# Seven small products for four of sixteen first-layer blocks per token group, and plain outputs for units 5 to 7

## The chip, the cores and the metric

The kernel runs on one core of a Trainium2 chip. The metric is the device time of one execution in microseconds (us). Before the change the median of 9 runs is 290.35 us, the lowest 289.78, the highest 291.69.

## What is computed

Retention (a linear attention with decay) over 8 batches, 8 heads, 576 positions and a head width of 64, followed by two matrix products with a leaky ReLU between them:

```
scores = q @ k^T / sqrt(64)
ret    = scores * D          # D[i,j] = gamma_h ** (i-j) for i >= j, else 0
x      = (ret @ v), heads side by side          # 4608 tokens x 512
h      = x @ w_in                               # 512 -> 2048
g      = max(0.01 * h, h)
out    = g @ w_out                              # 2048 -> 512
```

Inputs and output are float32; the kernel's matmuls take float16 operands and sum in float32.

## The kernel before, in words

**Units.** The tokens are cut into 36 units of 128 (two chunks of 64 positions). For each unit three tiles (k, q, v) are loaded; ScalarE casts k (`cast_k`, L170), VectorE or GpSimd multiply q and v by a decay table while they cast (`cast_q` L174, `cast_v` L177). q and k are transposed, for the first 8 units on TensorE (`transpose_pe`, `transposed`), later by a transposing DMA on SyncE's queue (`transpose_dma`, L181). `scores` (L209) makes the in-chunk scores and the chunk's state contribution; `masks` (L234) and `state` (L245) are VectorE's; `state_cast` (L273) makes the float16 state.

**Two forms of the outputs.** `outputs_acc` (L312) adds the in-chunk part and the part from the state in PSUM, in four rounds with a drain between, and ScalarE copies the sum into `xT` (`x_copy`, L346). `outputs` (L286) writes the two parts side by side; ScalarE copies one out (`own`, L359), and VectorE adds the other and writes `xT` (`add`, L365).

**Groups.** Four units are one group of 512 tokens (9 groups). `xT[g]` holds x transposed, 4 blocks of 128 features by 512 tokens. The first layer gives 16 blocks of 128 rows of `g`; one is `h_block` (L395): 4 matmuls of 512 columns (L379, in `h_mm`), then ScalarE's leaky ReLU (L393). `h_half` (L400) and `h_unit` (L407) make the same in pieces, for 256 and 128 tokens, while the first groups' units come in.

**The second layer.** Group 0's is written plainly (`wide`, L425, matmuls L429), with two output tiles `osb` of 256 tokens, stored by SyncE (`store`, L417). For groups 1 to 8, `seven` (L475) does it in Winograd's form of Strassen's scheme: tokens, hidden features and output columns are each halved, seven products (L493, 16 matmuls of 256 columns each) take the place of eight. The sums of the weights are made once (`mix_weights`, L446), those of `g` for every group by VectorE (`mix`, L461, instructions L473). The products p1, p6, p5 and p7 take a PSUM bank each, in this order; results are combined by `keep` (L502: ScalarE copy L505, VectorE sums L507) and `give` (L509: ScalarE copy L517, VectorE sums L519), which write two `osb` tiles per group.

**PSUM.** All of first layer, second layer and TensorE transposes share one pool of 4 banks (`acc_pool`, L80), handed out in turn; a bank's next user waits until the last reader of the one before is done. Scores and outputs have a tile each of their own.

**Order.** Every engine runs its instructions in the order in which the program writes them. There is no planner: the order is the text's. In the prologue (L600 to L646) fillers (`keep_warm`, L556: matmuls on a zero tile, nobody reads them) stand where TensorE waits. Then units 3 to 7 come in between pieces of groups 0 and 1 (L716 to L784). `burst(u)` (L682) is `scores(u)`, `outputs(u-1)`, `masks`, `state`, GpSimd's `state_cast`, `own(u-1)`, `add(u-1)`; `ahead(u)` (L697) is the three casts (q and v on GpSimd) and the transposing DMA; `step(u)` (L710) is `burst(u)`, the load of unit u+4 and `ahead(u+2)`. The main loop (L808 to L823) runs for groups 2 to 8: 16 blocks with a step after the 5th and the 13th and half of the mixes after the 9th, the other mixes, and `seven` with a step after its first and its fifth product.

**SyncE's queue.** Loads from unit 8 on, transposing DMAs and stores go out on it in program order.

Of the kernel before, what the change touches and what calls it, by code (L numbers as in the profile page):

```python
# [18 lines left out]
def kernel(  # L19
# [9 lines left out]
    nc = tc.nc  # L29
# [3 lines left out]
    P = 128  # L33
    CH = 64
    BLK = 256
    NP = H // 2
# [5 lines left out]
    HF, HN, HT = NF // 2, DM // 2, TOK // 2  # L42
# [30 lines left out]
    x_pool = ctx.enter_context(tc.tile_pool(name="xp", bufs=3))  # L73
    g_pool = ctx.enter_context(tc.tile_pool(name="gp", bufs=2))
    s_pool = ctx.enter_context(tc.tile_pool(name="sp", bufs=1))
    o_pool = ctx.enter_context(tc.tile_pool(name="op", bufs=3))
    m_pool = ctx.enter_context(tc.tile_pool(name="mp", bufs=1))
    sc_pool = ctx.enter_context(tc.tile_pool(name="scp", bufs=1, space=PSUM))
    ot_pool = ctx.enter_context(tc.tile_pool(name="otp", bufs=1, space=PSUM))
# [24 lines left out]
    w_in16 = const_pool.tile([P, NP, DFF], F16, name="w_in16")  # L104
    w_out16 = const_pool.tile([P, NF, DM], F16, name="w_out16")
    w_mix = const_pool.tile([P, 4, HF, HN], F16, name="w_mix")
    zst = const_pool.tile([P, NP, CH], F16, name="zst")
    idle = const_pool.tile([P, TOK], F16, name="idle")

# [9 lines left out]
    def load(u, eng=None, after=None):  # L119
        for x in (1, 0, 2):  # L120
            t = ld_pool.tile([P, H, D], FP, name=f"t32_{x}")
            t32[u, x] = t
            c = 2 * u
            same = c % CB + 1 < CB
            e = eng[x] if isinstance(eng, dict) else eng or nc.sync
            engs = e if isinstance(e, tuple) else (e,)
            n = H // len(engs)
            for j, rows in ((0, P),) if same else ((0, CH), (1, CH)):
                b, w = (c + j) // CB, (c + j) % CB
                for i, e in enumerate(engs):  # L130
                    hs = slice(n * i, n * i + n)
                    d = e.dma_start(
                        out=t[CH * j : CH * j + rows, hs],
                        in_=(q, k, v)[x][b, hs, CH * w : CH * w + rows, :].rearrange(
                            "h t d -> t h d"
                        ),
                    )
                    if after is not None and (x in after or not isinstance(after, dict)):
                        behind(d, *(after[x] if isinstance(after, dict) else after))
                        after = None  # L140
                    last_load[u, x] = d
# [32 lines left out]
    def cast_q(u, eng):  # L174
        eng.tensor_tensor(out=qk16[u][:, 0], in0=t32[u, 0], in1=decay(u, 0), op=MUL)  # L175

    def cast_v(u, eng):  # L177
        v16[u] = a_pool.tile([P, H, D], F16, name="v16")
        eng.tensor_tensor(out=v16[u], in0=t32[u, 2], in1=decay(u, 1), op=MUL)  # L179
# [54 lines left out]
    def masks(u):  # L234
        s16s[u] = b_pool.tile([P, 2, NP, CH], F16, name="s16")
        nc.vector.tensor_tensor(  # L236
            out=s16s[u],
            in0=sc_tiles[u][:, :, 0],
            in1=mask_sb.unsqueeze(1).unsqueeze(1).to_broadcast([P, 2, NP, CH]),
            op=MUL,  # L240
        )
# [117 lines left out]
    def own(u):  # L359
        owns[u] = b_pool.tile([P, NP, 2, CH], FP, name="own")  # L360
        nc.scalar.copy(  # L361
            out=owns[u], in_=ot_tiles[u][:, :, 0:NP].rearrange("q j c t -> q c j t")
        )
# [23 lines left out]
    def g_tile(g):  # L387
        if g not in g_t:
            g_t[g] = g_pool.tile([P, NF, TOK], F16, name="gt")
        return g_t[g]  # L390

    def leaky(out, in_):
        nc.scalar.activation(out=out, in_=in_, func=mybir.ActivationFunctionType.Lrelu)  # L393

    def h_block(g, f):  # L395
        hps = acc_pool.tile([P, 1, TOK], FP, name="acc")
        h_mm(hps, 0, g, f, slice(0, TOK))
        leaky(g_tile(g)[:, f : f + 1, :], hps)

    def h_half(g, a, fb):  # L400
        ts = slice(a * HT, (a + 1) * HT)
        hps = acc_pool.tile([P, 2, HT], FP, name="acc")
        for n in range(2):
            h_mm(hps, n, g, 2 * fb + n, ts)
        leaky(g_tile(g)[:, 2 * fb : 2 * fb + 2, ts], hps)

    def h_unit(u, fb):  # L407
        g, t0 = u // 4, (u % 4) * P
        ts = slice(t0, t0 + P)
        hps = acc_pool.tile([P, 4, P], FP, name="acc")  # L410
        for n in range(4):
            h_mm(hps, n, g, 4 * fb + n, ts)
        leaky(g_tile(g)[:, 4 * fb : 4 * fb + 4, ts], hps)

    def store(g, a, osb):  # L417
        r0 = g * TOK + a * HT
        nc.sync.dma_start(
            out=out[r0 : r0 + HT, :].rearrange("(t p) d -> p t d", p=P), in_=osb  # L420
        )
# [24 lines left out]
    def mix_weights(n, x):  # L446
        fs = slice(x * HF // 2, (x + 1) * HF // 2)
        a, b = (
            (w_part(0, 1), w_part(0, 0)),
            (w_part(1, 1), w_mix[:, 0]),  # L450
            (w_part(1, 1), w_part(0, 1)),
            (w_part(1, 0), w_mix[:, 1]),
        )[n]
        nc.vector.tensor_tensor(out=w_mix[:, n, fs], in0=a[:, fs], in1=b[:, fs], op=SUB)  # L454
# [101 lines left out]
    def keep_warm(n):  # L556
        t = acc_pool.tile([P, 1, TOK], FP, name="acc")
        for _ in range(n):
            nc.tensor.matmul(out=t[:, 0, :], lhsT=idle[:, 0:P], rhs=idle, start=True, stop=True)
# [76 lines left out]
    cast_q(3, nc.vector)  # L636
    cast_v(3, nc.vector)
    turn_act(3, 0)
    keep_warm(2)
    masks(2)  # L640
    scores(3)
    state_last(2)
# [6 lines left out]
    def halves(g, *items):  # L649
        for a, fb in items:  # L650
            h_half(g, a, fb)

    def cast_qv(u):
        cast_q(u, nc.vector)
        cast_v(u, nc.vector)

    def turn(u, x):
        transpose_pe(u, x)
        transposed(u, x, dve_copy)

# [36 lines left out]
    def ahead(u):  # L697

        if u >= NU:
            return  # L700
        cast_k(u)
        cast_q(u, nc.gpsimd)
        cast_v(u, nc.gpsimd)
        transpose_dma(u)
# [5 lines left out]
    def step(u):  # L710
        burst(u)
        fetch(u + 4)
        ahead(u + 2)


    halves(0, (0, 0), (0, 1))  # L716
    finish2(3)
    state_cast(3, act_copy, (1,))
    halves(0, (0, 2), (0, 3))
# [19 lines left out]
    scores(5)  # L739
    settle(5)  # L740
    cast_k(6)
    cast_qv(6)
    halves(0, (0, 6), (0, 7))
    finish(5)
    halves(0, (1, 6))
    turn(6, 1)
    cast_k(7)
    halves(0, (1, 7))
    turn(6, 0)
    cast_qv(7)  # L750
    h_unit(5, 0)
    scores(6)
    settle(6)
    h_unit(5, 1)
    turn(7, 1)
    halves(1, (0, 4))
    finish(6)
    turn(7, 0)
    halves(1, (0, 5))
    scores(7)  # L760
    settle(7)
    load(8, after=(w_out_loads[2],))
    load(9)
    halves(1, (0, 6), (0, 7))
    h_unit(6, 0)
    finish(7)
    h_unit(6, 1)
    mix_weights(0, 0)
    mix_weights(0, 1)
    h_unit(7, 0)  # L770
    h_unit(7, 1)
    mix_weights(1, 0)
    mix_weights(1, 1)
    halves(1, (1, 4))
    load(10)
    ahead(8)
    mix_weights(2, 0)
    mix_weights(2, 1)
    halves(1, (1, 5), (1, 6))
    ahead(9)  # L780
    load(11)
    mix_weights(3, 0)
    mix_weights(3, 1)
    halves(1, (1, 7))  # L784

    def early(u, n):
        burst(u)
        ahead(n)
        load(n + 2)
# [4 lines left out]
        3: lambda: mixes(1, 1),  # L794
        4: lambda: (burst(8, False), ahead(11), load(13)),
        7: lambda: mixes(1, 2),
        9: lambda: early(9, 12),
    }
    for n in range(16):
# [1 line left out]
        if n in at:  # L801
            at[n]()
    burst(10)
    seven(1, {0: [lambda: early(11, 13)], 4: [lambda: early(12, 14)]})

    first = [f for i in range(4) for f in (i, i + HF)]
    second = [f for i in range(4, 8) for f in (i, i + HF)]
    for g in range(2, NG):  # L808
        more = g < NG - 1
        for n, f in enumerate(first + second):  # L810
            h_block(g, f)
            if more and n in (4, 12):
                step(4 * g + 5 + (n == 12))
            if n == 8:
                for m in range(3):
                    mix(g, m, 0)
        for m in range(3):
            mix(g, m, 1)
        seven(
            g,  # L820
            {0: [lambda: step(4 * g + 7)], 4: [lambda: step(4 * g + 8)]} if more else {},
            g == NG - 1,
        )  # L823

# [29 lines left out]
```

## Time and profile before

| what | value |
|---|---|
| median of 9 runs | 290.35 us |
| the profiled execution | 291.11 us |
| its span in the profile | 289.30 us |
| TensorE busy | 280.3 us, 97% of the span |
| VectorE busy | 170.6 us, 59% |
| ScalarE busy | 144.5 us, 50% |
| GpSimd busy | 104.7 us, 36% |
| moved by DMA | 50.01 MB |
| one group in the middle (114.05 to 143.15) | 29.10 us, of which VectorE is busy 17.79 |

The page names the engines PE (TensorE matmul), PEld (its weight loads), DVE (VectorE), ACT (ScalarE), POOL (GpSimd) and SP (SyncE). The rows of slices cut the span into 40 equal parts of 7.2 us; a digit is the busy share in tenths. In a timeline each row is: start in us, duration in us, engine, line, operation, what it writes <- what it reads, shapes, how often; in brackets the idle time of the engine just before it and what ended it. Rows that follow each other with the same line and shapes are merged.

### The profile page before, as it was taken

The page shows a single profiled execution, that of the slowest core. Times are in us where ns is not written, and L with a number is a line of the kernel's source. Part 1 is how long each engine was busy: PE and PEld are TensorE (multiplying, and loading weights), DVE is VectorE, ACT ScalarE, POOL GpSimd, SP SyncE. Part 2 cuts the span into 40 slices and gives each one's busy share as a digit, 9 for nine tenths or more (in the row PEclk, how much of TensorE's full clock was granted, in tenths as well). Part 3 has the DMA queues.
Part 4 walks back from the last instruction along what each step waited for, and adds up shares of the span by engine and source line. Part 5 has one row for each costly group of instructions (what it writes and reads, how often), then busy time and mean ns, then how long its engine had stood idle before and what let it go on. Part 6 is the DMA issues. An engine that isn't in the chain of part 4 may idle for free.

```text
span 289.3 us, 9437 instructions
## 1 busy us (share of the span) xinstructions
PE 280.3 (97%) x4113; PEld 191.5 (66%) x4113; DVE 170.6 (59%) x294; ACT 144.5 (50%) x254; POOL 104.7 (36%) x124
## 2 busy tenths in 40 slices
PE   8699999999999999999999999999999999999994
PEld 3368888745874587458745874588448844884584
DVE  1885677864763495359635863686268636840352
ACT  4566766624327732773277317731773176307610
POOL 8869502763433324322524332234225413000000
PEclk9999999999999999999999999999999999999999
DMA  8999999998999987976797669766986151012003
GB/s 214 297 225 206 289 207 206 222 223 185 228 239 270 216 193 160 278 148 149 164 263 159 148 147 280 157 141 154 268 172 147 40 181 39 5 58 89 0 2 145
DMA packets 131738, 50.01 MB, mean 173 GB/s; under 512 B 121264, under 2 KB 126000, under 8 KB 131696
## 3 DMA queue, kind: packets, MB, share of 16 engines
q1 hardware_dynamic: 125392, 39.59, 58.3%
q0 software_dynamic: 6016, 9.70, 15.0%
q8 instruction: 32, 0.52, 0.8%
q10 hardware_dynamic: 288, 0.11, 0.1%
q14 instruction: 10, 0.08, 0.1%
HBM read 36.81 MB, written 9.44 MB: 160 GB/s over the span
## 4 chain that ended last, share of the span: by engine, by line
PE 91%; DVE 4%; DMA 2%; ACT 1%; issue 1%; POOL 0%; DVEq 0%; POOLq 0%
PE acc L379 43%; PE acc L493 34%; PE acc L429 5%; PE sc L218 3%; DMA t<-in_q_dram 2%; PE ot L294 1%; PE sc L227 1%; PE ot L305 1%; PE acc L200 1%; DVE qk L175 1%; DVE s L236 1%; PE ot L327 1%; DVE st L279 0%; DVE v L179 0%; ACT qkT L207 0%
## 5 line engine op out<-in xcount | busy, mean ns | idle before, releaser
L379 PE MATMUL acc<-xT,w_in 128*128 128x512 f16 (+2 forms) x768 | 130.9, 326 | 0.0
L393 ACT ACTIVATE gt<-acc 128x512 f16<-128x512 f32 x144 | 85.9, 598 | 56.2 <-PE acc L379 54.4
L379 PEld LDWEIGHTS <-w_in 128*128 128x128 f16 x768 | 68.2, 98 | 51.3
L493 PEld LDWEIGHTS <-gt 128*128 128x128 f16 x640 | 61.8, 98 | 9.1
L236 DVE TENSOR_TENSOR s<-sc,cs 128x512 f16<-128x512 f32 x34 | 23.3, 686 | 40.6 <-PE sc L227 40.6
L276 POOL CAST st<-s 128x512 f16<-128x512 f32 x21 | 12.8, 610 | 93.5 <-DVE s L260 57.9
L493 PE MATMUL acc<-w_out,gt 128*128 128x256 f16 x384 | 45.9, 273 | 0.2
L361 ACT COPY own<-ot 128x512 f32<-128x512 f32 x30 | 17.6, 586 | 42.8 <-PE ot L305 35.1
L175 POOL TENSOR_TENSOR qk<-t,cs 128x512 f16<-128x512 f32 x28 | 30.5, 1090 | 15.3 <-PE ot L327 14.8
L179 POOL TENSOR_TENSOR v<-t,cs 128x512 f16<-128x512 f32 x28 | 31.8, 1137 | 1.2 <-DVE w_mix L454 1.2
L473 DVE TENSOR_TENSOR mix<-gt 128x1024 f16<-128x1024 f16 x16 | 14.1, 879 | 29.8 <-ACT gt L393 29.8
L493 PE MATMUL acc<-w_mix,gt 128*128 128x256 f16 x256 | 30.6, 273 | 0.0
L493 PE MATMUL acc<-w_mix,mix 128*128 128x256 f16 x256 | 29.6, 273 | 0.0
L493 PEld LDWEIGHTS <-mix 128*128 128x128 f16 x256 | 25.0, 98 | 3.1 <-DVE mix L473 0.2
L172 ACT CAST qk<-t 128x512 f16<-128x512 f32 x36 | 22.3, 620 | 4.4 <-DMA t<-in_k_dram 4.4
L366 DVE TENSOR_TENSOR xT<-ot,own 128x512 f16<-128x512 f32 x30 | 20.5, 683 | 3.6 <-ACT own L361 3.6
L260 DVE TENSOR_TENSOR s<-sc,s 128x256 f32<-128x256 f32 x37 | 15.5, 420 | 2.4 <-PE sc L227 1.7
L218 PEld LDWEIGHTS <-qkT 64*64 64x64 f16 x576 | 7.9, 107 | 12.3 <-issue 11.2
L519 DVE TENSOR_TENSOR osb<-acc,u 128x512 f32<-128x512 f32 (+1 forms) x17 | 11.2, 657 | 7.9 <-PE acc L493 7.9
L473 DVE TENSOR_TENSOR mix<-mix,gt 128x1024 f16<-128x1024 f16 x16 | 14.8, 932 | 0.5
L279 POOL CAST st<-s 128x256 f16<-128x256 f32 x7 | 3.2, 454 | 31.4 <-DVE s L264 19.5
L429 PE MATMUL acc<-w_out,gt 128*128 128x512 f16 x64 | 14.3, 379 | 0.0
(60 smaller groups left out, 240.2 us busy)
## 6 DMA issues: line engine op xcount, KB each, us to landing
out_dram<-osb SPq DMA_DIRECT2D x17, 512.0 KB, 4.2
t<-in_k_dram SPq DMA_DIRECT2D x27, 256.0 KB, 4.0
t<-in_q_dram SPq DMA_DIRECT2D x26, 256.0 KB, 4.3
t<-in_v_dram SPq DMA_DIRECT2D x25, 256.0 KB, 4.9
w_in<-in_moe_w_in_dram POOLq DMA_DIRECT2D x8, 256.0 KB, 7.1
w_out<-in_moe_w_out_dram POOLq DMA_DIRECT2D x4, 512.0 KB, 10.5
t<-in_v_dram POOLq DMA_DIRECT2D x7, 256.0 KB, 6.5
t<-in_q_dram POOLq DMA_DIRECT2D x6, 256.0 KB, 6.2
```

The source lines that it names most:

```text
L172: nc.scalar.copy(out=qk16[u][:, 1], in_=t32[u, 1])
L175: eng.tensor_tensor(out=qk16[u][:, 0], in0=t32[u, 0], in1=decay(u, 0), op=MUL)
L179: eng.tensor_tensor(out=v16[u], in0=t32[u, 2], in1=decay(u, 1), op=MUL)
L218: nc.tensor.matmul(out=a[half(j), g, 0, p, :], lhsT=qkT[u][half(g), 1, p, half(j)], rhs=qkT[u][half(g), 0, p, half(j)], start=True, stop=T ...
L236: nc.vector.tensor_tensor(out=s16s[u], in0=sc_tiles[u][:, :, 0], in1=mask_sb.unsqueeze(1).unsqueeze(1).to_broadcast([P, 2, NP, CH]), op=MUL,)
L361: nc.scalar.copy(out=owns[u], in_=ot_tiles[u][:, :, 0:NP].rearrange("q j c t -> q c j t"))
L366: nc.vector.tensor_tensor(out=x_of(u).rearrange("q (c g) t -> q c g t", g=2), in0=ot_tiles[u][:, :, NP : 2 * NP].rearrange("q g (c j) t -> ...
L379: nc.tensor.matmul(out=hps[:, n, :], lhsT=w_in16[:, c, f * P : (f + 1) * P], rhs=xT[g][:, c, ts], start=(c == 0), stop=(c == NP - 1),)
L393: nc.scalar.activation(out=out, in_=in_, func=mybir.ActivationFunctionType.Lrelu)
L429: nc.tensor.matmul(out=ys[tb], lhsT=g_t[0][:, f, tb * P : (tb + 1) * P], rhs=w_out16[:, f, :], start=(f == 0), stop=(f == NF - 1),)
L473: nc.vector.tensor_tensor(out=z[:, fs], in0=a[:, fs], in1=b[:, fs], op=op)
L493: nc.tensor.matmul(out=r[name][tb][:, 0, :] if apart else r[name][0][:, tb, :], lhsT=lhs[:, f, tb * P : (tb + 1) * P], rhs=rhs[:, f, :], s ...
```

## The change

It has two parts.

*The first* is in the part where units come in. In the prologue two filler matmuls become the first block of group 0's first layer (`h_half(0, 0, 0)`), so unit 3's outputs follow one block later, not two. Units 5, 6 and 7 take the plain outputs (`finish2`) in place of the accumulating ones (`finish`). Around them the order is written anew: v casts and state casts stand in other places, two blocks of group 1 come after unit 7's outputs, and `ahead(8)` and the load of unit 10 are exchanged and moved one place forward.

*The second* computes blocks 0, 1, 8 and 9 of the first layer for groups 2 to 8 in the same seven-product form (`h_seven`), with halves of the input features, of the tokens, and the blocks 0, 1 against 8, 9. Each product is 4 matmuls of 256 columns. Four sums of `w_in` are made once (`sum_w_in`), four sums of `xT` for each group (`sum_x`, VectorE, 512 elements a partition each) near the end of the `seven` of the group before, behind its sixth product's result and ahead of the seventh's. Three ordinary blocks (`fill`) stand between the products. Four of the seven results go through VectorE sums (`plus`), then ScalarE's leaky ReLU reads them from SBUF. The ring of PSUM banks counts on: p1, fill, p6, p5, fill, p7, fill. In the loop the steps come after the first and the seventh of the nine remaining blocks, the half mixes after the fourth. The output tiles `osb` have two buffers, not three.

```diff
-    o_pool = ctx.enter_context(tc.tile_pool(name="op", bufs=3))
+    o_pool = ctx.enter_context(tc.tile_pool(name="op", bufs=2))
...
+    w_sum = const_pool.tile([P, 4, NP // 2, 2 * P], F16, name="w_sum")
...
+    def w_sub(i, j):
+        return w_in16[:, 2 * j : 2 * j + 2, i * HF * P : i * HF * P + 2 * P]
+
+    def x_sub(g, j, k):
+        return xT[g][:, 2 * j : 2 * j + 2, k * HT : (k + 1) * HT]
+
+    def sum_w_in(n):
+        a, b, op = (
+            (w_sub(1, 0), w_sub(1, 1), ADD),
+            (w_sum[:, 0], w_sub(0, 0), SUB),
+            (w_sub(0, 0), w_sub(1, 0), SUB),
+            (w_sub(0, 1), w_sum[:, 1], SUB),
+        )[n]
+        nc.vector.tensor_tensor(out=w_sum[:, n], in0=a, in1=b, op=op)
+
+    x_sums = {}
+
+    def sum_x(g):
+        x_sums[g] = t = s_pool.tile([P, 4, NP // 2, HT], F16, name="x_sum")
+        for n, (a, b) in enumerate(
+            (
+                (x_sub(g, 0, 1), x_sub(g, 0, 0)),
+                (x_sub(g, 1, 1), t[:, 0]),
+                (x_sub(g, 1, 1), x_sub(g, 0, 1)),
+                (x_sub(g, 1, 0), t[:, 1]),
+            )
+        ):
+            nc.vector.tensor_tensor(out=t[:, n], in0=a, in1=b, op=SUB)
+
+    def h_seven(g, fill):
+
+        r = {}
+        t = x_sums[g]
+
+        def product(name, lhs, rhs, fresh):
+            if fresh:
+                r[name] = acc_pool.tile([P, 2, HT], FP, name="acc")
+            for n in range(2):
+                for c in range(NP // 2):
+                    nc.tensor.matmul(
+                        out=r[name][:, n, :],
+                        lhsT=lhs[:, c, n * P : (n + 1) * P],
+                        rhs=rhs[:, c, :],
+                        start=fresh and n == 0 and c == 0,
+                        stop=c == NP // 2 - 1,
+                        skip_group_check=True,
+                    )
+
+        def plus(name, a, b):
+            r[name] = m_pool.tile([P, 2, HT], FP, name=name)
+            nc.vector.tensor_tensor(out=r[name], in0=r[a], in1=r[b], op=ADD)
+
+        def give(i, k, name):
+            leaky(g_tile(g)[:, i * HF : i * HF + 2, k * HT : (k + 1) * HT], r[name])
+
+        product("p1", w_sub(0, 0), x_sub(g, 0, 0), True)
+        r["k1"] = m_pool.tile([P, 2, HT], FP, name="k1")
+        nc.scalar.copy(out=r["k1"], in_=r["p1"])
+        h_block(g, fill[0])
+        product("p1", w_sub(0, 1), x_sub(g, 1, 0), False)
+        give(0, 0, "p1")
+        product("p6", w_sum[:, 1], t[:, 1], True)
+        plus("u2", "p6", "k1")
+        product("p5", w_sum[:, 0], t[:, 0], True)
+        plus("v", "p5", "u2")
+        h_block(g, fill[1])
+        product("p7", w_sum[:, 2], t[:, 2], True)
+        plus("h4", "p7", "v")
+        product("p5", w_sum[:, 3], x_sub(g, 1, 1), False)
+        plus("h5", "p5", "u2")
+        give(1, 1, "h4")
+        h_block(g, fill[2])
+        give(0, 1, "h5")
+        product("p7", w_sub(1, 1), t[:, 3], False)
+        plus("h6", "p7", "u2")
+        give(1, 0, "h6")
...
-    keep_warm(2)
+    h_half(0, 0, 0)
     masks(2)
...
-    halves(0, (0, 0), (0, 1))
+    halves(0, (0, 1))
     finish2(3)
...
-    cast_qv(6)
+    cast_q(6, nc.vector)
     halves(0, (0, 6), (0, 7))
-    finish(5)
+    finish2(5)
+    cast_v(6, nc.vector)
+    state_cast(5, act_copy, (1,))
     halves(0, (1, 6))
     turn(6, 1)
     cast_k(7)
     halves(0, (1, 7))
     turn(6, 0)
-    cast_qv(7)
     h_unit(5, 0)
     scores(6)
-    settle(6)
+    state(6, 0)
+    state_cast(6, dve_copy, (0,))
+    masks(6)
+    cast_q(7, nc.vector)
+    state(6, 1)
+    cast_v(7, nc.vector)
     h_unit(5, 1)
     turn(7, 1)
     halves(1, (0, 4))
-    finish(6)
+    outputs(6)
+    own(6)
     turn(7, 0)
+    add(6)
+    state_cast(6, act_copy, (1,))
     halves(1, (0, 5))
     scores(7)
     settle(7)
     load(8, after=(w_out_loads[2],))
     load(9)
+    h_unit(6, 0)
+    h_unit(6, 1)
+    finish2(7)
+    state_cast(7, act_copy, (1,))
     halves(1, (0, 6), (0, 7))
-    h_unit(6, 0)
-    finish(7)
-    h_unit(6, 1)
     mix_weights(0, 0)
     mix_weights(0, 1)
     h_unit(7, 0)
+    ahead(8)
+    load(10)
     h_unit(7, 1)
     mix_weights(1, 0)
     mix_weights(1, 1)
-    halves(1, (1, 4))
-    load(10)
-    ahead(8)
+    halves(1, (1, 4), (1, 5))
     mix_weights(2, 0)
     mix_weights(2, 1)
-    halves(1, (1, 5), (1, 6))
     ahead(9)
     load(11)
+    halves(1, (1, 6))
...
+        12: lambda: [sum_w_in(n) for n in range(4)],
...
-    seven(1, {0: [lambda: early(11, 13)], 4: [lambda: early(12, 14)]})
+    seven(1, {0: [lambda: early(11, 13)], 4: [lambda: early(12, 14)], 5: [lambda: sum_x(2)]})
...
+    rest = [f for i in range(2, HF) for f in (i, i + HF)]
     for g in range(2, NG):
         more = g < NG - 1
-        for n, f in enumerate(first + second):
+        h_seven(g, rest[:3])
+        for n, f in enumerate(rest[3:]):
             h_block(g, f)
-            if more and n in (4, 12):
-                step(4 * g + 5 + (n == 12))
-            if n == 8:
+            if more and n in (0, 6):
+                step(4 * g + 5 + (n == 6))
+            if n == 3:
                 for m in range(3):
                     mix(g, m, 0)
...
-            {0: [lambda: step(4 * g + 7)], 4: [lambda: step(4 * g + 8)]} if more else {},
+            {0: [lambda: step(4 * g + 7)], 4: [lambda: step(4 * g + 8)], 5: [lambda: sum_x(g + 1)]} if more else {},
```

More of the change, by code (lines that the diff above doesn't have):

```diff
@@ L803 @@
     burst(10)
-    seven(1, {0: [lambda: early(11, 13)], 4: [lambda: early(12, 14)]})
-    first = [f for i in range(4) for f in (i, i + HF)]
-    second = [f for i in range(4, 8) for f in (i, i + HF)]
+    seven(1, {0: [lambda: early(11, 13)], 4: [lambda: early(12, 14)], 5: [lambda: sum_x(2)]})
+    rest = [f for i in range(2, HF) for f in (i, i + HF)]
     for g in range(2, NG):
         more = g < NG - 1
-        for n, f in enumerate(first + second):
+        h_seven(g, rest[:3])
+        for n, f in enumerate(rest[3:]):
             h_block(g, f)
-            if more and n in (4, 12):
-                step(4 * g + 5 + (n == 12))
-            if n == 8:
+            if more and n in (0, 6):
+                step(4 * g + 5 + (n == 6))
+            if n == 3:
                 for m in range(3):
```

## The prediction, made before the changed kernel ran

> **What bounds the kernel now.** I read the page first (busy shares, slices, chain), then TensorE's timeline, then VectorE, GpSimd and SyncE beside it.
>
> ```profile
> span 289.3 us, 9437 instructions
> PE 280.3 (97%) x4113; PEld 191.5 (66%) x4113; DVE 170.6 (59%) x294; ACT 144.5 (50%) x254; POOL 104.7 (36%) x124
> PE   8699999999999999999999999999999999999994
> DMA  8999999998999987976797669766986151012003
> PE 91%; DVE 4%; DMA 2%; ACT 1%; issue 1%; POOL 0%; DVEq 0%; POOLq 0%
> ```
>
> TensorE is full from slice 3 on and carries 91% of the chain: a matmul saved is time saved, unless something new makes TensorE wait. The DMA row says that up to about 105 us the 16 engines are full as well, so there a transfer comes no sooner because TensorE is early. VectorE's 59% looks like room; it has to be read at the places where TensorE will wait for it.
>
> The seam between the second layer of one group and the first layer of the next (groups 3 and 4 here), from the timelines of TensorE, VectorE and GpSimd:
>
> ```profile
> 141.34 1.91 PE L493 MATMUL acc<-w_mix,gt 128*128 128x256 f16 x16
> 143.08 4.48 PE L379 MATMUL acc<-xT,w_in 128*128 128x512 f16 x20
> ...
> 141.64 0.68 DVE L519 TENSOR_TENSOR osb<-acc,u 128x512 f32<-128x512 f32 x1
> 143.28 0.69 DVE L519 TENSOR_TENSOR osb<-acc,u 128x512 f32<-128x512 f32 x1 [0.97 <-PE acc L493]
> ...
> 141.85 1.04 POOL L175 TENSOR_TENSOR qk<-t,cs 128x512 f16<-128x512 f32 x1
> 142.85 1.04 POOL L179 TENSOR_TENSOR v<-t,cs 128x512 f16<-128x512 f32 x1
> ```
>
> VectorE has a hole of 0.97 us between its last two results; exactly in it GpSimd casts the next unit's q and v. The change puts four additions into this hole.
>
> Does that collide? The mixes of before have two SBUF inputs, as the new sums have:
>
> ```profile
> 56.56 2.98 DVE L473 TENSOR_TENSOR mix<-mix,gt 128x1024 f16<-128x1024 f16 x2
> ...
> 130.10 1.23 DVE L473 TENSOR_TENSOR mix<-gt 128x1024 f16<-128x1024 f16 x1 [1.49 <-ACT gt L393]
> ...
> 56.07 1.48 POOL L175 TENSOR_TENSOR qk<-t,cs 128x512 f16<-128x512 f32 x1 [0.23 <-ACT gt L393]
> 57.51 1.49 POOL L179 TENSOR_TENSOR v<-t,cs 128x512 f16<-128x512 f32 x1
> ```
>
> A mix takes 0.69 alone. The one at 130.10 met a v cast that ran from 129.75 to 130.79 and ended at 131.33, 0.54 after the cast's end: it stood until the cast was over. At 56 us two mixes and two casts stretch each other to 1.49 apiece: mix and cast alternate, one whole instruction each.
>
> Last, SyncE's queue and the landing of one store:
>
> ```profile
> 76.21 0.82 SPq L132 DMA_DIRECT2D t<-in_v_dram  x1
> 77.13 2.15 SPq L419 DMA_DIRECT2D out_dram<-osb  x1
> 79.45 1.37 SPq L183 DMA_TRANSPOSE qkT<-qk  x1
> ...
> out_dram<-osb SPq DMA_DIRECT2D x1, 512.0 KB, 5.4
> ...
> 80.80 0.69 DVE L519 TENSOR_TENSOR osb<-acc,v 128x512 f32<-128x512 f32 x1 [1.05 <-PE acc L493]
> ```
>
> Group 0's second store is ready at 70.8 (its ACT copy) but stands behind loads, and lands at 77.13 + 5.4 = 82.5.
>
> **What the Trainium skill says.** "SBUF — State Buffer", section "Who interferes with whom": a VectorE instruction with two SBUF inputs contends with a GpSimd instruction that reads SBUF; the later one blocks until the earlier is through. The trace agrees (0.54 after the cast's end). "VectorE: DVE Perf Modes", "The perf-mode tier table": tensor_tensor has a doubled rate for 16 bits in SBUF, the plain one with a PSUM operand. The trace agrees: 0.69 for 1024 f16 elements and for 512 from PSUM. "TensorE: Matmul & The Clock Gate", "Back-to-back issue gap": 518 cycles for 512 columns, 262 for 256; here 2.60/12 = 0.2167 us (97.56 to 100.16) and 3.50/32 = 0.1094 (81.35 to 84.85). "DMA: Bandwidth & Descriptors", "Queues, rings and completion order": descriptors are consumed in ring order; with SyncE issuing back to back here, the store can't overtake the loads.
>
> **Part 1, the prologue's filler and units 5 to 7.** Two fillers (0.43 us) go and a first-layer block of 8 x 0.1094 = 0.87 comes in. It can start when unit 1's x copy ends (17.34), finishes near 18.25, and pushes unit 3's scores from 17.92 to 18.28; unit 3's outputs come at about 20.3, not 20.92: 0.6 gained. Plain outputs take 0.37 (20.92 to 21.29), the accumulating form 0.9 (36.00 to 36.90), so 3 x 0.52 = 1.56 gained, for three ACT copies in the place of three others and three VectorE additions of 0.60. VectorE pays in its order: unit 6's addition and unit 7's v cast stand by the copies of unit 7's transposes; by my walk the last copy ends at 43.4 where TensorE wants unit 7's scores at 42.8, and unit 6's first-layer blocks wait 0.2 for its addition. Sum: about -1.65 at the start of group 0's second layer (55.0); bounds -1.0 (more such waits) and -2.2 (none). The moved K and V issues: unit 8's transpose now precedes unit 10's load on SyncE; it is ready at 50.3, the load goes 51.7 and unit 11's load 57.4, as before (57.37), since the DMA engines are the limit.
>
> **Part 2, one output buffer less.** With three, the first group of the seven-product form finds a free buffer, and its second waits for a store long landed. With two, the VectorE result at 80.80 - 1.65 = 79.15 goes into the buffer of the store that lands at 82.5. VectorE's queue is in order: behind it stand masks, states and the addition for unit 11, the next result, the four sums, the last result. ScalarE's copy for the first buffer waits likewise until 70.78 + 5.5 = 76.3, with nothing urgent behind it. So part 1's gain is swallowed here whatever its size: VectorE starts 82.55, ends 83.24, the product that adds into the same bank starts 83.28 (before: 83.11). Later groups have over 10 us between store and reuse: nothing.
>
> **Part 3, seven small products for four blocks.** Per group 16 x 0.2167 - 28 x 0.1094 = 0.40 saved, 7 groups: -2.8. ScalarE keeps four evictions and gets one copy; VectorE gets five PSUM additions (0.60 apart, 0.74 when dependent) and four sums. A sum is 512 elements: half of the mix's data time, 0.27, and 0.335 apart (0.60 - 0.27); one dependent 0.46. Inside the seven, the chain of additions just keeps ahead of TensorE (second p5 product wanted 1.75 after p6 ends, v ready 1.65 after), so nothing there; bounds 0 to 0.1 a group.
>
> The wait is at the bank of product p5: in a ring of four it is the fourth bank since the previous seven's p7, which the last VectorE result frees, and this result now stands behind the four sums. p5 is wanted 0.437 x 3 + 0.867 = 2.18 after the first layer's start H. The sums: the first stands until the q cast ends, takes 0.27; the v cast gets in with 0.91 (152.25 to 153.16 after a mix); the other three end 0.27 + 2 x 0.335 later; the result ends 0.61 after them (it starts 0.08 before the last one's end, and lasts 0.69); 0.04 to TensorE. So p5 starts at q's end + 2.77, a stall of (q's end - H) + 0.59. From the traces q's end - H is -0.19 at groups 2, 3 and 6, +0.33 at 4, +0.27 at 5: stalls 0.40, 0.40, 0.40, 0.92, 0.86, together 2.98. After group 7 no cast runs: none. Bounds: 0 if the sums slip in ahead, 1.2 each if another cast gets in.
>
> The steps (scores, outputs, masks, states, casts, loads, transpose) move within the group: the first comes 7.0 us after H, not 4.4, the second 12.9, the third 17.1; the transpose that the first issues goes some 3.6 later (GpSimd's two casts ahead of it), lands within 3.6 more (99 to 105 us), and is wanted two steps on, 10 us later: nothing, 1 us if one lands late (5.8 was seen). The mixes now meet the casts of the first and second step and stand some 2 us on VectorE; what waits for them is the seven's second product, due 2 us later still: nothing, and D below if that cover goes.
>
> At group 1 both waits add: all is 1.75 later (82.55 against 80.80), q ends 86.83, p5 starts 89.60, against 84.85 + 2.18 = 87.03 before: +2.57.
>
> **Sum.** +2.57 (part 1 and both waits) - 7 x 0.40 + 2.98 = +2.75. The sums of w_in (4 x 0.335, once) fall into VectorE's idle 3.85 us before 70.6: nothing; if that cover were gone, 1.5. The profiled execution took 291.11 (span 289.30 and 1.81 around it), so 293.86 for such a one; the median of the runs is 0.76 lower: **293.1**.
>
> **Rivals.** (B) The casts don't stand in the sums' way: place the seam, price 1.2 to 1.7 us of VectorE time, deciding once the last result ends within 2.14 of H. Without casts the sums last 1.47; at group 1 p5 starts 88.4, +1.4; later stalls vanish: 1.4 - 2.8 = -1.4, 288.9, faster. For it: the hole; against: 130.10. (C) The store lands before 79: part 1 stays, group 1 stalls 0.82: -1.65 + 0.82 + 2.98 - 2.8 = -0.65, 289.7. For it: the DMA row has some slack (0.89 from 65 to 70); against: SyncE's unbroken queue. (D) VectorE becomes the bound: 17.7 us a group (114 to 143) + 1.5 + 3.3 + about 4 of standing = 26.5 of 29; 0.3 more in each of 7 groups, +4.9: 295.2. (E) Neither wait appears: -4.5, 285.9.
>
> **Chances.** Forecast 0.62, D 0.10, B 0.12, C 0.11, E 0.05. The forecast's own range is 291.5 to 294.7 (landing +-0.7, order of casts). Range of all 289.0 to 295.0. 0.2% (0.6 us) is about what can be told from no change: faster by more 0.23 (B, E, half of C), same 0.07, slower 0.70.
>
> **What would show it.** Right: VectorE's first `osb<-acc,v` waits for a DMA until near 82.5; at the seams `x_sum` is 0.3 to 1.3 long with GpSimd beside it, and TensorE stands 0.4 to 0.9 ahead of the third small product, except at the last group. Wrong: `x_sum` 0.35 throughout (B), or that result near 79 (C). Part 1: second layer of group 0 at 53.4.

## The result, and the profile after

The changed kernel takes 295.81 us (median of 9 runs, 294.60 to 297.61) against 290.32 (28 runs): a ratio of 1.0193 [1.0173, 1.0213], 5.5 us slower. The forecast was 293.1 and "slower": the sign held, the size was half. The profiled execution took 297.32, 2.12 of it outside the span. One run of one later kernel, with the stores on ScalarE's queue, was in a slower state of the chip and is left out of its numbers.

The page of the changed kernel: the span, the shares of the engines, the slices of TensorE and DMA, and the chain.

```profile
span 295.2 us, 9709 instructions
PE 279.0 (95%) x4195; PEld 198.6 (67%) x4195; DVE 224.2 (76%) x364; ACT 145.1 (49%) x261; POOL 110.1 (37%) x124
PE   6889999999959999999999999999999999999995
DMA  8999999998997997948694979397949451003004
PE 62%; DVE 16%; DMA 7%; POOL 5%; SPq 4%; issue 3%; ACT 1%; DVEq 0%; ACTq 0%; POOLq 0%
```

TensorE's work went down (280.3 to 279.0), its share of the chain from 91% to 62%. VectorE, DMA, GpSimd and SyncE's queue now hold 32% of it (before: VectorE 4% and DMA 2%), and one slice of TensorE's row (the twelfth, 81 to 89 us) shows a hole.

The hole, in the timelines of SyncE's queue, VectorE and TensorE:

```profile
79.40 1.24 SPq L499 DMA_DIRECT2D out_dram<-osb  x1
84.77 0.69 DVE L599 TENSOR_TENSOR osb<-acc,v 128x512 f32<-128x512 f32 x1 [6.80 <-DMA out_dram<-osb]
85.52 2.42 PE L573 MATMUL acc<-w_mix,gt 128*128 128x256 f16 x16 [3.32 <-DVE osb L599]
```

VectorE stands (is idle) for 6.80 us until group 0's second store has landed, and TensorE 3.32 behind it: the wait that the prediction named, but 2.2 us later than it put it (82.55).

An ordinary seam (into group 3), VectorE, GpSimd and TensorE:

```profile
117.47 0.94 DVE L445 TENSOR_TENSOR x_sum<-xT 128x512 f16<-128x512 f16 x1
118.45 1.15 DVE L445 TENSOR_TENSOR x_sum<-xT,x_sum 128x512 f16<-128x512 f16 x1
119.52 0.41 DVE L445 TENSOR_TENSOR x_sum<-xT 128x512 f16<-128x512 f16 x1
...
120.19 0.68 DVE L599 TENSOR_TENSOR osb<-acc,u 128x512 f32<-128x512 f32 x1
117.09 1.04 POOL L176 TENSOR_TENSOR qk<-t,cs 128x512 f16<-128x512 f32 x1
118.09 1.22 POOL L180 TENSOR_TENSOR v<-t,cs 128x512 f16<-128x512 f32 x1
...
120.92 0.60 PE L457 MATMUL acc<-x_sum,w_sum 128*128 128x256 f16 x4 [0.25 <-DVE osb L599]
```

The first sum ends 0.28 after the q cast, the second 0.29 after the v cast; the other two, with nothing beside them, take 0.41. The last result of VectorE slips behind them, and the product p5, which wants that result's bank, starts at 120.92. The prediction's rule (end of q's cast + 2.77) gives 118.13 + 2.77 = 120.90.

### The profile page after: what moved, and what is told of

It reads as the page before. It is cut to its first block, busy times and chain, and to the rows that moved or that the text cites. A ratio compares the mean times of both kernels' runs of the same rounds, so it can differ in the third digit from the quotient of the medians.

```text
span 295.2 us, 9709 instructions
## 1 busy us (share of the span) xinstructions
PE 279.0 (95%) x4195; PEld 198.6 (67%) x4195; DVE 224.2 (76%) x364; ACT 145.1 (49%) x261; POOL 110.1 (37%) x124
## 2 busy tenths in 40 slices
DMA packets 131739, 50.03 MB, mean 169 GB/s; under 512 B 121264, under 2 KB 126000, under 8 KB 131696
## 4 chain that ended last, share of the span: by engine, by line
PE 62%; DVE 16%; DMA 7%; POOL 5%; SPq 4%; issue 3%; ACT 1%; DVEq 0%; ACTq 0%; POOLq 0%
PE acc L380 30%; PE acc L573 24%; DVE x_sum L445 5%; PE acc L457 4%; DVE osb L599 4%; DMA t<-in_v_dram 3%; SPq L133 3%; POOL t L133 3%; DMA w_in<-in_moe_w_in_dram 2%; DMA out_dram<-osb 2%; DVE xT L367 2%; SPq L184 2%; DVE s L237 1%; PE sc L219 1%; ACT k L585 1%
## 5 line engine op out<-in xcount | busy, mean ns | idle before, releaser
L380 PE MATMUL acc<-xT,w_in 128*128 128x512 f16 (+2 forms) x656 | 111.1, 318 | 0.4 <-DMA w_in<-in_moe_w_in_dram 0.2
L394 ACT ACTIVATE gt<-acc 128x512 f16<-128x512 f32 x123 | 72.4, 596 | 32.4 <-PE acc L380 31.7
L380 PEld LDWEIGHTS <-w_in 128*128 128x128 f16 x656 | 57.4, 98 | 34.6 <-issue 0.9
L180 POOL TENSOR_TENSOR v<-t,cs 128x512 f16<-128x512 f32 x28 | 35.6, 1272 | 1.2 <-DMA t<-in_v_dram 1.1
L367 DVE TENSOR_TENSOR xT<-ot,own 128x512 f16<-128x512 f32 x33 | 22.5, 683 | 5.0 <-ACT own L362 4.9
L553 DVE TENSOR_TENSOR mix<-gt 128x1024 f16<-128x1024 f16 x16 | 16.5, 1037 | 9.0 <-ACT gt L394 9.0
L553 DVE TENSOR_TENSOR mix<-mix,gt 128x1024 f16<-128x1024 f16 x16 | 18.2, 1142 | 0.5
L475 ACT COPY k<-acc 128x512 f32<-128x512 f32 x7 | 4.1, 585 | 25.0 <-issue 21.5
L599 DVE TENSOR_TENSOR osb<-acc,v 128x512 f32<-128x512 f32 (+1 forms) x9 | 5.7, 633 | 13.2 <-DMA out_dram<-osb 6.8
L394 ACT ACTIVATE gt<-h 128x512 f16<-128x512 f32 x21 | 13.2, 627 | 4.8 <-DVE h L468 4.5
```

The lines of the kernel that those rows point to most:

```text
L367: nc.vector.tensor_tensor(out=x_of(u).rearrange("q (c g) t -> q c g t", g=2), in0=ot_tiles[u][:, :, NP : 2 * NP].rearrange("q g (c j) t -> ...
L380: nc.tensor.matmul(out=hps[:, n, :], lhsT=w_in16[:, c, f * P : (f + 1) * P], rhs=xT[g][:, c, ts], start=(c == 0), stop=(c == NP - 1),)
L553: nc.vector.tensor_tensor(out=z[:, fs], in0=a[:, fs], in1=b[:, fs], op=op)
L599: nc.vector.tensor_tensor(out=to, in0=r[of][n], in1=r[plus][:, ts], op=ADD)
```

## The experiments

Each kernel was timed beside the kernel before on the same chip, where that took 290.38, 290.40 or 290.71 us; the ratios are to it. Lines of diffs are against the changed kernel unless said otherwise.

**First theory.** The loss is two waits of about equal size, the store and the casts. A rival: something else that both hide.

*Three output buffers.* The space for the third comes from letting two of the sums in `plus` share a tile.

```diff
-    o_pool = ctx.enter_context(tc.tile_pool(name="op", bufs=2))
+    o_pool = ctx.enter_context(tc.tile_pool(name="op", bufs=3))
...
-            r[name] = m_pool.tile([P, 2, HT], FP, name=name)
+            r[name] = m_pool.tile([P, 2, HT], FP, name="h4" if name == "h6" else name)
```

> The changed kernel with three output buffers again (room for it: h6 shares h4's tile). Theory 1 (the wait for group 0's second store, which lands at 84.7 us, carries the excess): VectorE's first result of group 1 no longer waits for a store; the stand of 3.3 us ahead of the seventh product and the half clock behind it are gone; group 3 starts near 112.6 us and not at 118.3; time 290.1 us, equal to before. Theory 2 (the seams and a slower TensorE carry it, the store is covered): 294 to 296 us.

Measured: 290.53 (290.42 to 291.42), ratio 1.0017 [1.0007, 1.0026]: 5.3 less than the changed kernel. VectorE's result, in the timeline of this kernel:

```profile
78.94 0.69 DVE L599 TENSOR_TENSOR osb<-acc,v 128x512 f32<-128x512 f32 x1 [1.05 <-PE acc L573]
```

It waits for its product alone. The store itself goes out no earlier (79.13). So the missing buffer carries about 5.3 us. Not all of that is this wait: of the 6.25 between the two profiled executions, 5.38 is there when group 3 starts (118.32 for 112.94), 0.50 comes between there and group 8, and 0.35 lies outside the span.

*The sums behind the last result*, two buffers.

```diff
-    seven(1, {0: [lambda: early(11, 13)], 4: [lambda: early(12, 14)], 5: [lambda: sum_x(2)]})
+    seven(1, {0: [lambda: early(11, 13)], 4: [lambda: early(12, 14)], 6: [lambda: sum_x(2)]})
...
-            {0: [lambda: step(4 * g + 7)], 4: [lambda: step(4 * g + 8)], 5: [lambda: sum_x(g + 1)]} if more else {},
+            {0: [lambda: step(4 * g + 7)], 4: [lambda: step(4 * g + 8)], 6: [lambda: sum_x(g + 1)]} if more else {},
```

> The changed kernel with the four sums of xT behind the last result of the second layer, not ahead of it; two buffers stay. Theory 1 (GpSimd's two casts stand in the sums' way, and the bank waits for the result behind them): the stands of 0.4 to 0.9 us at five seams go, but for about 0.2 at two of them; time 292.5 us. Theory 2 (the stands come from VectorE being full, wherever the sums are): same as the changed kernel, 295.8 us.

Measured: 292.56 (292.41 to 293.78), ratio 1.0094 [1.0070, 1.0119]: 3.2 less. On VectorE the result now leads, and the sums behind it meet no cast:

```profile
115.51 0.69 DVE L599 TENSOR_TENSOR osb<-acc,u 128x512 f32<-128x512 f32 x1 [0.97 <-PE acc L573]
116.12 0.41 DVE L445 TENSOR_TENSOR x_sum<-xT 128x512 f16<-128x512 f16 x1
```

At two seams, into groups 5 and 6, the first sum still meets the v cast (0.81 and 0.75), and TensorE stands 0.23 and 0.16, as expected. In the profiles some 2.2 us of the gain are the seams: 0.35 from VectorE's waiting result to group 3, and 1.81 from there to group 8 (145.39 for 147.20). The store also landed earlier here, at 82.11.

*Both edits.*

> Three buffers and the sums last together. If the two waits are the whole of the loss, this keeps part 1 (1.8 us) and most of part 3 (2.8 us less 0.1 a group): 286.5 to 287 us, faster than before. If a third cost is there (VectorE full, the mixes against the casts), 289 us or more.

Measured: 288.87 (287.56 to 289.50), ratio 0.9947 [0.9924, 0.9970]. Faster than before, but by less than the two gains add to, and not the 286.5 to 287 of the theory. In its profile the stretch from group 0's second layer to group 2's first (52.83 to 84.12) lasts 31.29. TensorE stands there for units whose transposes landed late:

```profile
71.12 0.32 PE L219 MATMUL sc<-qkT 64*64 64x64 f16 x16 [0.59 <-DMA qkT<-qk]
79.98 0.32 PE L219 MATMUL sc<-qkT 64*64 64x64 f16 x16 [0.24 <-DMA qkT<-qk]
```

A third stand (0.63, for a state cast) lies between these two.

*Part 1 alone*: the kernel before with the changed prologue and entry of units 3 to 7, nothing of the second part.

> The kernel before with the first part of the change alone (filler block, plain outputs, the order of units 5 to 7 with the transpose of unit 8 ahead of the load of unit 10); three buffers, no small products. Theory 1: the 1.8 us gained at the start of group 0's second layer stay to the end: 288.5 us. Theory 2 (they are given back in the stretch in which the DMA engines are full, up to 105 us, for the transfers come no sooner): 290.3 us.

Measured: 289.13 (288.56 to 290.25), ratio 0.9969 [0.9953, 0.9985]: part 1 is worth some 1.25. The same stretch lasts 29.85 here, without these stands.

**Second theory.** The late store and the 1.4 us longer stretch have one cause: the change puts unit 8's transpose ahead of unit 10's load in SyncE's queue, so that later items wait for casts of late loads. A rival: chance, or the DMA engines.

*The old order of that queue*, two buffers.

```diff
     h_unit(7, 0)
-    ahead(8)
-    load(10)
     h_unit(7, 1)
...
-    halves(1, (1, 4), (1, 5))
+    halves(1, (1, 4))
+    load(10)
+    ahead(8)
     mix_weights(2, 0)
     mix_weights(2, 1)
+    halves(1, (1, 5))
```

> The changed kernel, two output buffers, with unit 10's load again ahead of unit 8's casts and transpose, and both again behind the block of group 1, as before the change. Theory (the exchange made every later item of SyncE's queue wait for casts of late loads, and so put group 0's second store 2.2 us later): the store's issue comes back to 76.5 to 77.2 and lands near 82.5, VectorE's first result of group 1 starts near 82.6, the first layer of group 2 near 85.6 to 86.1, and the time is 293.3 to 293.8. Rival (the store is late for another cause, the DMA engines or the later steps): 295.8, store still near 79.4.

Measured: 296.09 (4 runs, 295.07 to 297.75), ratio 1.0200 [1.0148, 1.0251]. In the profile (295.52) the store went out earlier, at 77.97, though not in the 76.5 to 77.2 of the theory, and then TensorE stood for something else:

```profile
82.95 0.69 DVE L599 TENSOR_TENSOR osb<-acc,v 128x512 f32<-128x512 f32 x1 [4.48 <-DMA out_dram<-osb]
88.75 1.05 PE L457 MATMUL acc<-x_sum,w_sum 128*128 128x256 f16 x8 [1.15 <-DVE x_sum L445]
91.64 0.60 PE L457 MATMUL acc<-xT,w_sum 128*128 128x256 f16 x4 [0.54 <-DVE v L468]
```

TensorE is released sooner and then stands for the sums: VectorE carries the path all the way. The profile speaks in part for the theory, the runs against it; undecided.

*Three buffers, sums last, old order.*

> Three output buffers, the sums of x behind the last result, and the old order of unit 10's load and unit 8's transpose. Theory (the third cost, some 1.4 us between the start of group 0's second layer and the first layer of group 2, comes from that order): 287.3 to 287.9, with that stretch 29.9 long, not 31.3. Rival (it comes from the seven-product part or from plain outputs making units early): 288.9, stretch 31.3.

Measured: 289.67 (20 runs, 288.09 to 292.16), ratio 0.9969 [0.9948, 0.9991]: no better than with the new order. The stretch is 29.87, as the theory has it, but group 0's second layer starts at 54.61, because this execution began badly. TensorE's timeline, and its windows (stretch, its length, PE busy, granted clock, DMA share, GB/s):

```profile
7.90 0.40 PE L201 MATMUL acc<-ident,qk 128*128 128x128 f16 x4 [1.98 <-DVE qk L176]
```

```profile
7.00:14.00 7.00, 5.94 (x103) 0.76 1.07 307
```

A late cast keeps TensorE waiting, half clock follows, and everything after is some 1.8 later. Of the 20 runs, the 7 with a mean granted clock of 0.994 or less all took 289.75 or more; the other 13 have a median of 288.97, as both edits have in the new order (288.87, clocks of 0.998 or more). The 20 runs leave the theory no support beyond this one stretch.

*The exchange alone*: `load(10)` ahead of `ahead(8)` at the place of the change.

```diff
     h_unit(7, 0)
-    ahead(8)
     load(10)
+    ahead(8)
```

> The changed kernel with only unit 10's load again ahead of unit 8's casts and transpose; their place in the order of the other engines stays as changed. Theory (the exchange alone puts group 0's second store later): store issued at 76.5 to 77.5, first layer of group 2 at 85.4 to 86.2, and 1.5 to 2.3 less than the changed kernel run beside it. Rival (the place, or chance from run to run, moves the store): no difference beyond 0.5 from the changed kernel run beside it.

*The changed kernel once more*, beside it.

> The changed kernel once more, beside the others of this call: 295.8, with the second store issued at 78.5 to 79.8. If the store's issue moves by 1.5 or more between two executions of the same program, the time of landing is partly chance.

Measured: 295.19 (295.04 to 295.88) with the exchange undone, 295.04 (294.25 to 296.29) as changed. No difference: the theory of the queue's order falls. The second run of the changed kernel issued the store 0.47 sooner than the first (78.93 for 79.40), and VectorE's result started 1.06 sooner (83.71 for 84.77), less than the 1.5 that I had set as proof of chance.

*The second part alone*: prologue and entry of before, two buffers.

> The prologue and the entry of the units as before the change, with the seven small products and two output buffers. Theory (with two buffers VectorE waits for group 0's second store, so what part 1 gains is swallowed; in the old order of SyncE's queue the store lands near 82.5 whatever TensorE does): the second layer of group 0 starts at 55.0, the first layer of group 2 at 85.4 to 86.0, and the profiled execution is within 0.6 of that of the kernel with the old order of the queue alone (295.5). Rival (part 1 is worth its 1.7 here as well): first layer of group 2 at 87 or later, 297 or more.

Measured: 294.46 (4 runs, 292.59 to 296.82), ratio 1.0130 [1.0085, 1.0175]. The landing is the latest of all (85.14), in the old order, so the expectation of 82.5 failed. The first layer of group 2 starts at 89.20, where the rival had it, but because of this landing and not because part 1 came through. In time it does not differ from the whole change by more than the runs scatter: with two buffers part 1's gain does not come through.

All profiles of kernels that wait for the store, with the start of group 3's first layer in each:

| kernel | order of queue | store issued | VectorE's result starts | group 3 starts | difference |
|---|---|---|---|---|---|
| forecast | | 77.13 | 82.55 | 116.14 | 33.59 |
| changed | new | 79.40 | 84.77 | 118.32 | 33.55 |
| changed, again | new | 78.93 | 83.71 | 117.25 | 33.54 |
| exchange undone | old | 78.38 | 83.34 | 116.89 | 33.55 |
| old order | old | 77.97 | 82.95 | 116.50 | 33.55 |
| second part alone | old | 79.48 | 85.14 | 118.69 | 33.55 |
| sums behind the result | new | 77.35 | 82.11 | 115.31 | 33.20 |

(The forecast's start of group 3 is 113.97, as before, plus 2.57, less 0.40.) With the kernels that do not wait, 13 profiles have the issue between 76.65 and 79.81: 77.13 to 79.48 in the old order, 76.65 to 79.81 in the new. Order does not sort them. Seven of the 13 share one program up to this store and differ only behind it and in the number of buffers: the changed kernel twice (79.40, 78.93), the sums behind the result (77.35), three buffers alone (79.13), both edits (79.81), and the two with moved casts that follow below (76.65, 77.42). They spread as far as all 13, and three of them on one chip (77.35, 79.13, 79.81) by 2.46, so no difference in the program ahead of the store is needed for it. With three buffers the longer stretch goes with the late store: 31.29 and 30.63 where it is issued at 79.81 and 79.13, 29.85 and 29.84 where it is at 76.65 and 77.42.

*Group 0's stores on ScalarE's queue*, two buffers.

```diff
-        nc.sync.dma_start(
+        (nc.scalar if g == 0 else nc.sync).dma_start(
```

> The changed kernel with group 0's two stores issued from ScalarE's queue, the rest as changed: two output buffers. Theory (it is not the number of buffers but the store's place in SyncE's queue that makes VectorE wait): the second store goes out at about 71, lands before 79, VectorE's first result of group 1 waits for no DMA, and the time is 290.0 to 290.6 as with three buffers. Rival (the DMA engines are full, the store lands as late from any queue): store lands after 82 and the time is 293 or more.

Measured: 291.33 (19 runs, 290.37 to 294.66), ratio 1.0046 [1.0024, 1.0068], 0.7 above the range that was expected. The wait is gone:

```profile
69.65 0.42 ACTq L499 DMA_DIRECT2D out_dram<-osb  x1
...
79.53 0.69 DVE L599 TENSOR_TENSOR osb<-acc,v 128x512 f32<-128x512 f32 x1 [1.06 <-PE acc L573]
```

The same buffers and bytes, issued about ten microseconds sooner. The Trainium skill, "DMA: Bandwidth & Descriptors", section "Issuing engines are not separate DMA queues", says that another issuing engine saves only the sequencer's time to start the DMA, usually small beside the DMA itself, since all end on the same 16 engines. Here the issue is what counted: in SyncE's queue the store stood behind loads and transposes and went out 9.75 us later, for a DMA that took 5.4 to land (79.40 to 84.77).

**Third theory.** GpSimd's casts stretch the sums, not the sums' number. The sums-last run doesn't tell these apart, since it moves the sums from in front of the result as well.

*Casts written behind the last result*, three buffers (group 1's `seven` likewise).

```diff
...
-            {0: [lambda: step(4 * g + 7)], 4: [lambda: step(4 * g + 8)], 5: [lambda: sum_x(g + 1)]} if more else {},
+            {0: [lambda: step(4 * g + 7)], 4: [lambda: (burst(4 * g + 8), fetch(4 * g + 12))], 5: [lambda: sum_x(g + 1)], 6: [lambda: ahead(4 * g + 10)]} if more else {},
```

> The changed kernel with three output buffers, the sums of x where the change put them, and the casts, load or transpose of the last step of each group moved behind the last result. Theory (the casts on GpSimd are what stretches the sums): all four sums take 0.41 or less, TensorE stands nowhere ahead of the third small product, and the time is 287.3 to 288.0. Rival (four sums ahead of the last result are too long by themselves): stands of 0.4 stay and the time is 290.0 to 290.6.

Measured: 290.54 (290.17 to 291.87), ratio 1.0003 [0.9985, 1.0021], and this decides nothing: the edit did not part them. GpSimd and VectorE in this kernel:

```profile
112.34 1.23 POOL L180 TENSOR_TENSOR v<-t,cs 128x512 f16<-128x512 f32 x1
112.70 1.15 DVE L445 TENSOR_TENSOR x_sum<-xT,x_sum 128x512 f16<-128x512 f16 x1
```

Each engine has a queue of its own; a later place in the text moved the casts behind nothing on GpSimd's, so they ran at the same time as ever. To keep them out of the way they have to come *sooner*.

*Casts one stage sooner*, three buffers (group 1's `seven` likewise).

```diff
...
-            {0: [lambda: step(4 * g + 7)], 4: [lambda: step(4 * g + 8)], 5: [lambda: sum_x(g + 1)]} if more else {},
+            {0: [lambda: step(4 * g + 7)], 2: [lambda: ahead(4 * g + 10)], 4: [lambda: burst(4 * g + 8), lambda: fetch(4 * g + 12)], 5: [lambda: sum_x(g + 1)]} if more else {},
```

> The changed kernel with three output buffers; the casts and the transpose that the last step of each group issues come one stage sooner, behind the third of the seven products, so that GpSimd is through with them before the sums begin; the sums stay where the change put them. Theory (the casts are what stretches the sums): GpSimd stands idle beside the sums, all four take 0.41 or less, TensorE stands nowhere ahead of the third small product, the groups last 28.8 to 28.9, and the time is 287.3 to 288.2. Rival (four sums ahead of the last result are too long by themselves): stands of 0.25 and 0.66 stay, groups of 29.2 to 29.7, and the time is 290.0 to 290.6.

Measured: 287.30 (287.09 to 287.32), ratio 0.9880 [0.9854, 0.9906]: 3.1 to 3.4 faster than before, the fastest of all. VectorE, GpSimd and TensorE at the seam:

```profile
110.85 0.41 DVE L445 TENSOR_TENSOR x_sum<-xT 128x512 f16<-128x512 f16 x1
111.30 0.42 DVE L445 TENSOR_TENSOR x_sum<-xT,x_sum 128x512 f16<-128x512 f16 x1
...
112.31 0.68 DVE L599 TENSOR_TENSOR osb<-acc,u 128x512 f32<-128x512 f32 x1
108.67 1.05 POOL L180 TENSOR_TENSOR v<-t,cs 128x512 f16<-128x512 f32 x1
...
113.45 1.04 PE L457 MATMUL acc<-x_sum,w_sum 128*128 128x256 f16 x8
```

The casts are over at 109.7, all sums are short although they stand in front of the result, and the products p6 and p5 run in one piece (x8). Against three buffers alone this is 3.2 us: the price of the collision, with nothing else moved but the k cast and the transpose that go with these casts, and the load, still behind its burst. The profiles put 3.2 on the seams as well: 0.41 from group 2's start to group 3's, and 2.75 from there to group 8 (143.95 for 146.70). The stretch from group 0's second layer to group 2's first is 29.84, in the *new* order of the queue: the longer stretch of the kernel with both edits was not the order either.

## Why the prediction was right in sign and wrong in size

*The failed step: the landing of one store.* The prediction took "lands at 77.13 + 5.4 = 82.5" from one execution of before, and held it nearly fixed ("unit 11's load 57.4, as before (57.37), since the DMA engines are the limit"; own range "landing +-0.7"). In the changed kernel unit 11's load did go out at 57.72, but the store at 79.40, and VectorE's result started at 84.77, not 82.55. Over six profiles of kernels that wait for it, it started from 82.11 to 85.14, five of them later than forecast, 83.67 on the mean. I had taken for good within 0.7 a time whose issue lies anywhere in 3.2 us over 13 profiles of nearly the same program, and the one that I read (77.13) is the second earliest. The seven profiles with the same program up to the store show that it moves this far from one execution to another; whether the change also shifts its mean stays open, and no effect of the queue's order is seen.

*Sum against the profiled execution*: 297.32 for 293.86, 3.46 too little.

| term | too little by |
|---|---|
| store: group 3 starts at 118.32, not 116.14 | 2.18 |
| the five groups from there to group 8 (147.20, not 145.30 - 5 x 0.40 + 2.98 = 146.28) | 0.92 |
| from group 8's start to the end (29.68, not 30.03 - 0.40) | 0.05 |
| outside the span (2.12, not 1.81) | 0.31 |

The profiled execution of the changed kernel lay 1.51 above its median (that of before 0.76), so 2.7 of the 3.46 show in the medians. By the mean landing of 83.67 the first term would be 1.1. The last term is no scatter: in the kernels with two buffers and the new entry of the units every run has 2.09 to 2.26 outside the span, in all others, the second part alone with its two buffers too, 1.73 to 1.88. Why, the runs do not say.

*The seam after the landing was right to 0.05*: the table's last column, where the sums stand in front (33.54 or 33.55 for 33.59). From VectorE's result on, all is VectorE's time, in every kernel with the sums in front. That is also why the clock did not matter. After its 3.32 us of standing, TensorE ran at half clock for 3.4 us:

```profile
87.00:88.00 1.00, 1.00 (x7) 0.50 1.18 270
...
90.00:91.00 1.00, 1.00 (x10) 0.91 0.84 194
```

(The columns are as above.) The Trainium skill, "TensorE: Matmul & The Clock Gate", section "Part 1: The HAM clock gate", has half rate after an idle window of about 3.4 us that runs freely. The traces agree on the half rate, but none of the stands here was as long as that window: those of 3.32, 3.13 and 2.77, and the 1.98 in the execution that began badly, came with 0.50, for 3.41 or 3.42 us each time; one of 2.83 and one of 1.72 did not. Here page and measurement differ, and the measured stands decide. Group 3 starts 33.55 after the result with or without it.

*The later seams* are as forecast. Counted from the first layer's start, as the prediction counts, p5 comes at 2.61 where 2.18 + 0.40 was expected, at 3.13 for 2.18 + 0.92 and at 3.06 for 2.18 + 0.86. Of the 0.92 that the groups lost beyond it, 0.08 in each of four groups is mostly the second layer's second product, which starts 0.33 after its step and not 0.28 (135.96 to 136.29 against 160.69 to 160.97 in before), held by ScalarE's copy of the first; 0.23 in group 6 is the second product into p5's bank waiting for the sum v, in the chain of additions that I had put at 0 to 0.1. Another 0.36, in group 7, stands at the same copy:

```profile
254.57 1.91 PE L573 MATMUL acc<-w_out,gt 128*128 128x256 f16 x16 [0.36 <-ACT k L585]
```

With three buffers groups 6 and 7 last 29.65 and 28.93, not 29.89 and 29.21: of these two waits only the usual 0.08 is there. So it is in the second part alone, which has two buffers. Why they are longer here the runs do not say.

*What the small products save* was over-sized: groups without stands last 28.85 against 29.11, 0.26 less, not 0.40. In the kernel with early casts TensorE starts the second product into p5's bank 0.49 after the one ahead (0.44 elsewhere), and the second layer's second product 0.05 later behind its step (0.33 for 0.28), together 0.11 of the 0.14. Seven groups give 1.8; with part 1's 1.25 that is the 3.1 by which the best version beats before.

*Part 1*: forecast 1.65, measured 1.25 when alone, inside its bounds. In the changed kernel group 0's second layer starts at 53.17, forecast 53.4. One trace cannot price it more closely: with the old prologue group 0's second layer started at 54.99 in one profile and 53.81 in another.

*The rivals.* B (casts not in the way) falls with the early casts: they are worth 3.2. C (store lands before 79) falls in every two-buffer kernel but the one with the stores on another queue. D (VectorE as the bound) falls: at 76% of the span, the same share as in the changed kernel, the early-cast version has no stand over 0.16 us after group 0's first layer; it is the place of VectorE's work that counted, not its amount. The time of 295.81 lies near D's 295.2, by luck and for another reason. E (neither wait) is what the early-cast kernel builds: 287.3, not 285.9, since both savings were put too high.

## What to carry to other kernels

Before a buffer is given up, look at what its last user's DMA stands behind in its queue, and treat a landing time from one profile as a draw: take its spread over several executions before building a sum on it. Two-input VectorE work and GpSimd work that fall into the same short gap should be parted by moving the free one earlier; a later place in the program moves nothing on a queue that is empty. A change with two good halves (1.25 and 1.8 us) lost 8.5 through one buffer (5.3) and one collision (3.2), and each of these could be undone in a few words.

## What was not expected of the hardware

The same 512 KB store, behind the same program, was issued anywhere within 3.2 us (76.65 to 79.81). The four runs of the early-cast kernel lie within 0.23 us of each other (287.09 to 287.32), the nine of the changed kernel within 3.0 (294.60 to 297.61), though both move the same bytes (50.03 MB). The wait for the store is not all of this scatter: the kernel with three buffers, the sums last and the old order waits for no store, and its 20 runs lie within 4.1.
